# Sparse attention and a mixture of attention experts on one core: another order for all 766 steps

## The chip, the core and the metric

The kernel runs on one core of a Trainium2 chip. A core has five engines that run side by side, each through its own queue in order: TensorE (PE; its weight loads are shown as PEld), VectorE (DVE), ScalarE (ACT), GpSimd (POOL) and SyncE (SP), which only issues transfers here. DMA engines move data between memory and the core's SBUF; matmuls write to PSUM, eight banks of 512 fp32 per partition. The metric is the device time of one execution in microseconds (us). The profile comes from one execution; the times from three others.

## What is computed

```python
def _attn_ref(q, k, v):                 # (4, 8, 768, 64): batch, heads, positions, width
    block, window = (32, 16)
    k_sum = k.reshape(B, H, nb, block, D).max(axis=3)
    v_sum = v.reshape(B, H, nb, block, D).mean(axis=3)
    scores_l = scale * q @ k.T          # kept where |i - j| < window
    scores_s = scale * q @ k_sum.T + log(block)
    a = softmax(concat(scores_l_masked, scores_s))
    return a @ concat(v, v_sum)

def _moe_ref(x, w_gate, wq, wk, wv, wo):  # x: (4, 768, 512), E = 4 experts, 64 wide
    logits = x @ w_gate                   # the two largest of four, softmax over them
    for e in range(E):
        q, k, v = x @ wq[e], x @ wk[e], x @ wv[e]
        a = softmax(causal(scale * q @ k.T))
        out += weight_of(e) * (a @ v @ wo[e])
```

The second function takes the first one's output, heads side by side.

## The kernel before

The work is cut into 766 steps. `make_plan` declares them: a step has a name, the engines that it can run on, the buffers that it reads and writes, and a function that records its instructions. `TABLE` (from line 55) gives the order: each entry is a step's number, the engine that it runs on (P, V, A, G, S for PE, DVE, ACT, POOL, SP) and the slots of the buffers that it uses first. `Plan.emit` walks the table; so the table alone sets the order of every engine's queue, which copy of a tile or which PSUM bank a step uses, and through these every wait. `SLOTS` (line 51) says how many copies each tile has; PSUM has eight banks, and many steps take two at once.

Names of steps carry the batch b (0 to 3) and the pair of heads c (0 to 3), and for the second stage the pair of experts (0, 1) and a part. By pair of heads, in the first stage:

- dk, dq (POOL, lines 261 and 266) load k and q; dv (SP, lines 284 to 287) loads v into one of six `vb` tiles, in overlapping windows; hc copies the overlap within the tile.
- bs (line 304) sums v over blocks with matmuls against the selector `sel`, be adds up the parts and ds spreads the sums into `vb`. For the second half of the batches dvs loads v again and tr adds it up in a tree on POOL (line 347) in their place.
- tk and tq turn k and q with transposes on PE (line 366); kw and cq take them out of PSUM; rk takes the maximum over blocks and ksc spreads it.
- sc forms the scores (lines 414 and 420, the first adds the mask), ex takes the exponential on ACT (line 427), av multiplies by v (line 437), rc and xm divide (lines 448 and 452), tx turns the result (line 463), hi and lo keep it as a sum of two half-precision tiles (lo at line 482).

In the second stage, for a batch:

- vp forms v of all experts and the gate's logits (lines 554 and 557); v2 and lg take them out of PSUM; ga, gx, gb, gc work out the gate (lines 595 to 614).
- pp forms q and k of a pair of experts (line 630) and pc takes them out; sp forms a unit of scores (line 654), es takes the exponential (line 662, ACT), dm puts zeros above the diagonal (line 667, POOL), aw multiplies by v (line 678).
- r2 and wv divide and weigh (lines 697 to 704), tw turns (line 715), ct copies the turned tile `wT`, op multiplies by the output weights (line 737), oc takes the result out of PSUM into `ob`, od stores it (line 748).

The first stage of one batch is mixed with the second stage of the batch before it. The weights are loaded once (dw, dwv, dwo, dwg) and cast (cw, cvg, co, cg). 24 fillers fl (line 769) are steps that read zeros: on PE they are one or four matmuls of 512 columns, on ACT they record nothing. `vone`, `knz`, `kwz`, `id16`, `id32`, `idr`, `sel`, `mt`, `pi`, `vtz`, `v2o`, `zz` and `w1m` set constants before first use.

PE works in one of four array shapes: 128 rows by 128 columns (pp, vp, aw, op, fl), 64 by 128 (sc, sp, tx, tw), 128 by 64 (tk, tq, av; rows 100, 128 and 120 in the profile) and 128 by 32 (bs; 96 rows).

Plain copies and casts of all steps are recorded at line 168 when they run on ACT and at line 170 when they run on another engine, so one line of the profile holds many steps.

Of the kernel before, what the change touches and what calls it, by code (L numbers as in the profile page):

```python
# [15 lines left out]
S = 768  # L16
# [41 lines left out]
75,P,4.1 57,G, 56,A, 73,V, 94,P,6.0 232,G,2 49,P,5.1 72,V, 95,A, 67,G, 96,P,0.1 76,A, 126,P,2.2 50,V, 148,G, 74,A,  # L58
97,A, 77,P,6.2 127,A, 41,V,4 99,P,4.0.0 78,A, 109,P,3.0 234,S,4 68,P,2.0 51,A, 243,G,1 98,P, 69,V, 44,G, 62,G, 110,A,
105,P,0.2.2 79,P,6.3 236,S,3 107,V, 122,P,1.0.0 80,A, 70,G, 81,P,2.1.1 124,V, 106,A, 82,P, 100,V, 108,G, 101,V, 123,A,  # L60
233,G,2 252,P,6.1.1 83,V, 125,G, 111,P,4.4 84,V, 253,A, 0,G, 63,P,7.1 144,S,0 112,A, 128,P,0.5 64,V, 130,P,2.1 129,A,
143,S, 102,P,4.0.0 254,V, 131,A, 142,S,1 65,G, 113,P,0.0 269,P,7.0.2 103,V, 141,S, 132,P,2.0.2 270,A, 242,G,0 140,S,
104,V, 114,A, 145,S, 237,G, 271,V, 133,P, 85,P,4.1.1 235,G, 134,V, 135,V, 115,P,0.1.0 86,A, 116,P, 1,A, 87,V, 45,G,
136,P,6.2.2 117,V, 273,P,2.1 118,V, 137,A, 307,P,3.2 238,P,4.0 272,A, 138,V, 274,A, 150,G, 308,A, 275,P,0.2 239,V,
46,G, 119,P,6.3.3 276,A, 244,S,0 277,P,2.3 286,P,5.2.0 120,A, 240,G, 256,P,4.0 287,V, 278,A, 196,P,0.0 255,A, 241,G,
257,A, 288,V, 194,P,2.1 246,S,2 197,A, 121,V, 289,G, 149,G, 303,P,4.0.2 195,A, 290,P,5.1 304,V, 260,P,0.5 147,A,
204,P,6.0 408,S,0 279,P,2.0.1 406,S, 261,A, 305,V, 409,S, 280,P, 245,G, 205,A, 407,S, 152,P,0.0.0 402,S,3 281,V,
282,V, 291,A, 258,P,6.1 154,A, 283,P,4.4.4 259,A, 247,G, 153,V, 201,P,2 284,V, 202,A, 146,S, 306,G, 248,P,0.1 285,V,
401,G,1 203,G, 210,P,6 249,V, 198,P,2 263,P,4.1.2 199,A, 262,P, 251,G, 211,A, 165,P,0.2 404,S,4 264,V, 265,V, 415,G,2
# [12 lines left out]
226,P,4.4 230,A, 590,G,1 346,P,0.1 227,V, 343,P,6 347,A, 386,P,1.0.2 425,G,0 384,P, 344,A, 228,S, 385,P, 337,P,4
387,V, 604,P,0.1.0 338,A, 388,V, 349,P,6 466,P,1.2 350,A, 606,V, 352,P,4 427,G, 456,P,2.0.2 597,S,0 353,A, 467,V,
340,P,6 389,P,4.0 341,A, 455,P, 390,V, 345,G, 348,G, 483,P,1.1 605,A, 592,S,4 354,G, 457,V, 439,P,4.1.0 458,V, 465,G,
351,G, 438,P, 484,A, 339,G, 38,G,1 482,A, 468,P,6.2 440,V, 470,P,2.4 441,V, 469,A, 625,P,0.0 621,P,1.0.2 471,A, 626,V,
342,G, 487,P,6.0 580,S,1 426,G, 459,P,4.0.0 488,A, 622,V, 485,P,2.3 608,P,0.2 486,A, 355,P,0.1.6 607,G, 623,V, 357,P,
609,A, 593,G, 594,S,3 356,P, 460,A, 612,P,2.1 358,V, 489,P,0.0.1 417,G, 359,V, 613,A, 490,P, 461,V, 588,G, 360,P,2.1
624,A, 598,S, 442,P,6.1.1 596,S, 361,V, 629,P,4.5 231,S, 443,A, 491,V, 472,P,2.1.2 492,V, 599,S, 9,G, 630,A, 473,P,
444,V, 610,P,0.3 595,G, 493,P,4.2.2 474,V, 611,A, 475,V, 394,P,6.0 494,V, 579,G, 397,P,0.4 395,A, 495,V, 476,P,2.3.3
591,G,0 396,S, 391,P,6.2 477,A, 398,V, 540,P,4.1 392,A, 478,V, 399,S, 538,P,0.0 393,S, 541,A, 600,G, 627,P,6.0 539,V,  # L90
655,P,2.2.1 628,A, 638,P,3.1.0 656,V, 551,P,4.0 548,P,0 552,A, 589,G, 499,P,6.0.0 657,V, 549,A, 509,P,4.2 500,V,
601,G,0 639,V, 501,A, 554,P,0 510,A, 545,P,6 640,V, 642,P,2.1 555,A, 502,P,4 643,V, 546,A, 641,G, 496,P,0 553,G,
504,V, 550,G, 503,V, 581,G, 557,P,2 542,P,6 497,V, 498,V, 558,A, 644,P,4.2 543,A, 615,P,2.0.0 505,V,0.0 507,V, 614,P,
# [808 lines left out]
```

## Time and profile before

| | us |
|---|---|
| three runs | 165.97, 166.53, 166.67 |
| median | 166.53 |
| profiled execution | 162.94 |
| its span, from the first to the last instruction | 161.2 |
| PE busy in it | 143.5 |
| ACT busy | 119.5 |
| DVE busy | 116.8 |
| POOL busy | 109.9 |

The busy share of an engine is an average over the span. The slices of the page cut the span into 40 parts of 4.03 us; the chain follows the work that ended last back to the beginning. A row of grouped instructions has line, engine, operation, the tiles out<-in, their shapes, the count, then the busy time in us and the mean of one in ns, then the idle time of the engine before them and what ended it. A row of a timeline begins with the start in us and the length in us. The ends of matmuls are modelled: a matmul is shown as ending up to 0.17 us after the next one has begun.

### The profile page before, as it was taken

Reading aid. Unit: us, or ns where it says so; the run is one execution under the profiler, and the core shown is the slowest. Engines: PE = TensorE matmul, PEld = TensorE weight load, DVE = VectorE, ACT = ScalarE, POOL = GpSimd, SP = SyncE. Lnnn points to the kernel's source line nnn. Section 1 sums busy time; section 2 is a strip of 40 time slices with the busy share of each in tenths; the row PEclk is TensorE's granted clock in tenths of the full one; section 3 lists DMA queues with packets and bytes.
Section 4 is the critical chain, followed back from the end, with each engine's and each line's share of the span. In section 5 each row is a group of like instructions: output and inputs, shape, how many; then the busy total and the mean of one; then the engine's idle time right before and its main releaser. Section 6 shows DMA issues by size and latency. Waiting matters only on the chain.

```text
span 161.2 us, 6956 instructions
## 1 busy us (share of the span) xinstructions
PE 143.5 (89%) x2992; PEld 107.1 (66%) x2992; DVE 116.8 (72%) x236; ACT 119.5 (74%) x152; POOL 109.9 (68%) x184
## 2 busy tenths in 40 slices
PE   0049998769999999999999999998999998999994
PEld 0137796758687778577666988656778795466741
DVE  5527488985878967977786899968888578247940
ACT  0096999566996779898889997639788894999460
POOL 6987595984874999999999989649996230216100
PEclk9999999999999999999999999999999999999999
DMA  3999999997889996998799985699200000030746
GB/s 21 215 226 237 188 161 232 222 218 166 173 170 186 237 157 151 176 168 129 181 173 166 266 151 119 188 268 267 81 0 4 4 6 0 4 130 0 257 167 231
DMA packets 44158, 24.57 MB, mean 152 GB/s; under 512 B 33120, under 2 KB 40544, under 8 KB 43744
## 3 DMA queue, kind: packets, MB, share of 16 engines
q1 hardware_dynamic: 35552, 16.91, 43.7%
q0 software_dynamic: 7488, 6.29, 28.0%
q10 hardware_dynamic: 1088, 0.93, 1.7%
q8 instruction: 23, 0.38, 1.0%
q14 instruction: 7, 0.06, 0.1%
HBM read 24.13 MB, written 6.29 MB: 189 GB/s over the span
## 4 chain that ended last, share of the span: by engine, by line
PE 69%; ACT 12%; POOL 5%; issue 4%; DMA 4%; SPq 2%; DVE 2%; POOLq 0%; ACTq 0%; DVEq 0%
PE ps L437 13%; PE ps L630 12%; PE ps L554 6%; PE ps L678 6%; PE ps L654 6%; PE ps L366 6%; PE ps L737 4%; DMA out_dram<-ob 4%; PE ps L304 4%; PE ps L414 3%; PE ps L463 3%; ACT a L662 3%; PE ps L420 3%; ACT aT L427 2%; ACT kw L168 2%
## 5 line engine op out<-in xcount | busy, mean ns | idle before, releaser
L662 ACT ACTIVATE a<-ps 128x1024 f16<-128x1024 f32 (+1 forms) x48 | 41.7, 919 | 6.9 <-PE ps L654 4.9
L667 POOL TENSOR_SCALAR_AFFINE_SELECT a<-a 128x256 f16<-128x256 f16 x48 | 18.3, 406 | 22.1 <-ACT a L662 21.6
L427 ACT ACTIVATE aT<-ps 120x768 f32<-120x768 f32 x32 | 25.3, 812 | 4.5 <-PE ps L420 3.1
L437 PE MATMUL ps<-vb,aT 120*64 120x65 f32 x768 | 26.5, 224 | 1.3 <-issue 0.9
L437 PEld LDWEIGHTS ps<-vb,aT 120*64 120x64 f32 x768 | 24.1, 138 | 4.0 <-issue 2.4
L630 PE MATMUL ps<-hi,wqk 128*128 128x384 f16 x128 | 22.8, 326 | 0.3 <-ACT ob L168 0.3
L170 POOL COPY vb<-vb 32x1408 f32<-32x1408 f32 x15 | 20.1, 1350 | 3.7 <-DMA vb<-in_v_dram 3.1
L347 POOL TENSOR_TENSOR vt<-vt 120x1024 f32<-120x1024 f32 (+3 forms) x16 | 19.2, 1201 | 3.5 <-DMA vt<-in_v_dram 2.4
L630 PEld LDWEIGHTS <-wqk 128*128 128x128 f16 x128 | 11.7, 97 | 8.3 <-issue 1.0
L482 DVE TENSOR_TENSOR lo<-ps,hi 128x768 f16<-128x768 f32 x16 | 15.3, 955 | 1.3 <-ACT hi L168 0.8
L382 DVE TENSOR_REDUCE ks<-ps 128x24 f16<-128x768 f16 x16 | 15.0, 951 | 1.2 <-PE ps L366 1.0
L366 PE MATMUL ps<-idr,kn 100*64 100x100 f16 x256 | 8.9, 219 | 7.8 <-POOL idr L225 7.7
L452 DVE TENSOR_TENSOR x<-ps,rec 128x768 f32<-128x768 f32 x16 | 15.3, 958 | 0.6
L654 PE MATMUL ps<-qk,qk 64*128 64x512 f16 (+3 forms) x128 | 14.5, 307 | 0.7 <-ACT qk L168 0.4
L554 PE MATMUL ps<-wvg,hi 128*128 128x264 f16 x96 | 13.9, 276 | 0.1
L170 POOL COPY vb<-vu 24x768 f32<-24x768 f32 x16 | 13.1, 822 | 0.8
L366 PEld LDWEIGHTS <-kn 100*64 100x64 f16 x256 | 7.3, 117 | 9.0 <-DVE vb L210 5.6
L168 ACT COPY ob<-ps 128x1024 f32<-128x1024 f32 (+1 forms) x9 | 8.5, 968 | 6.1 <-PE ps L737 3.9
L170 POOL COPY vb<-vs 24x1536 f32<-24x1536 f32 x6 | 8.7, 1467 | 5.9 <-DVE vs L322 5.8
L678 PE MATMUL ps<-v,a 128*128 128x65 f16 x336 | 12.1, 193 | 0.0
L737 PE MATMUL ps<-wo,wT 128*128 128x512 f16 (+1 forms) x50 | 11.7, 371 | 0.4 <-DVE wT L170 0.4
L678 PEld LDWEIGHTS <-a 128*128 128x128 f16 x336 | 11.0, 97 | 1.5 <-issue 0.8
(95 smaller groups left out, 276.9 us busy)
## 6 DMA issues: line engine op xcount, KB each, us to landing
vb<-in_v_dram SPq DMA_DIRECT2D x32, 176.0 KB
out_dram<-ob SPq DMA_DIRECT2D x10, 512.0 KB
vt<-in_v_dram SPq DMA_DIRECT2D x16, 192.0 KB
kn<-in_k_dram POOLq DMA_DIRECT2D x6, 384.0 KB, 6.8
qn<-in_q_dram POOLq DMA_DIRECT2D x6, 384.0 KB, 6.6
kn<-in_k_dram POOLq DMA_DIRECT2D x4, 192.0 KB, 5.2
qn<-in_q_dram POOLq DMA_DIRECT2D x4, 192.0 KB, 5.9
a<-in_moe_wk_dram SPq DMA_DIRECT2D x2, 256.0 KB
```

What stands on the lines that cost most here:

```text
L170: en(e).tensor_copy(dst, src)
L347: en(e).tensor_tensor(y[0:120], x[0:120, 0:w], x[0:120, w:2 * w], AL.add)
L366: nc.tensor.transpose(dst[64 * hp:64 * hp + 64, p * s:p * s + p], src[:, hh + hp, 64 * s:64 * s + 64], idt)
L427: nc.scalar.activation(T["aT"][aT.slot][0:KR], pbank(sc, 2)[0:KR, :, 0:384], AF.Exp, scale=SCALE)
L437: nc.tensor.matmul(pbank(av, 2)[o:o + 64, u, 65 * (2 * (t // 2) + hp):65 * (2 * (t // 2) + hp) + 65], a[0:KR, hp, 64 * t:64 * t + 64], T[" ...
L554: nc.tensor.matmul(p[:, i, 0:264], hi_(ch)[:, cols], T["wvg"][:, ch, :], start=(ch == 0), stop=False, skip_group_check=True)
L630: nc.tensor.matmul(pbank(pp, 2)[:, u, 0:384], T["wqk"][:, cc, ch, j, :], hi_(ch)[:, 384 * u:384 * u + 384], start=(ch == 0), stop=(ch == N ...
L654: nc.tensor.matmul(pbank(sp, 2)[:, ep, c0:c0 + w], T["qk"][qk[1].slot][r, 128 * tj:128 * tj + 128], T["qk"][qk[0].slot][r, n0:n0 + w], sta ...
L662: nc.scalar.activation(a2v(u), pbank(sp, 2)[:, :, 0:ln], AF.Exp, scale=SCALE / (XS * XS))
L667: nc.gpsimd.affine_select(m, m, [[0, 2], [1, 128]], AL.is_ge, 0.0, base=0, channel_multiplier=-1)
L678: nc.tensor.matmul(pbank(av, 2)[:, ep, 65 * ti:65 * ti + 65], a2v(u)[:, ep, o:o + 128], T["v2"][v2.slot][:, tj, 2 * cc + ep, :], start=(tj ...
L737: nc.tensor.matmul(pbank(op, i1 - i0)[:, ti - i0, 0:n1 - n0], T["wT"][wTs[cc].slot][:, 128 * ti:128 * ti + 128], T["wo"][:, cc, n0:n1], st ...
```

## The change

Only the table is replaced. All 766 steps are there in both; every one of the lines differs. The first and the last lines:

```diff
 TABLE = """
-4,G,0 139,A, 40,V,3 2,G, 8,V, 52,S,3 39,G,2 35,G, 47,S,2 3,G,0 42,V,5 5,G, 58,G,1 6,G, 66,S,5 7,G, 34,V, 37,G,0
-88,P,0.0.0 53,A, 90,V, 60,G, 89,A, 59,G,1 61,S,0 43,G, 91,G, 54,P,1.0 36,G, 92,P,2.0 55,V, 48,G, 71,P,3.1.1 93,A,
...
-763,P,4.3 758,A, 23,P,5 761,V, 30,P,6 764,V, 29,P,7 759,A, 17,P,0 765,S, 16,A,1 762,A, 27,A,5 24,A,2 33,A,3 31,A,6
-14,A,7 15,A,4 18,A,1 32,A,1 13,A,1 28,A,1 21,P,1 22,P,2 19,P,3 10,P,4
+4,G,0 37,V,0 2,G, 5,G,0 40,V,3 52,S,0 3,G, 39,V,2 41,G,4 8,V, 47,S,3 57,G,1 59,G, 6,G, 43,G, 34,V, 66,S,2 7,G, 36,G,
+88,P,0.0.0 53,A, 90,V, 35,G, 58,G,1 42,G,5 91,A, 54,P,1.0 89,A, 71,P,2.1.1 55,V, 61,S,5 48,G, 92,P,3.0 73,V, 75,P,4.1
...
+717,V, 29,A,5 24,A,4 33,A,4 20,A,4 750,A, 26,P,4 30,A,5 18,A,5 757,P,5.6 756,S, 760,P,4.2 758,A, 763,P,6.3 28,P,7
+25,P,2 761,A, 764,V, 23,P,3 759,A, 19,P,0 765,S, 10,P,1 21,A,5 22,A,7 12,A,2 32,A,4 14,A,6 762,S, 15,P,3 17,P,2 13,P,4
 """
```

What the two tables say by engine, read with the names of the steps:

| queue | before | after |
|---|---|---|
| PE, begin | tk01 bs01 tq01 tk00 tq00 sc010 bs00 sc011 tq03 sc000 av011 | tk01 bs01 tk00 tq01 tq00 sc010 sc011 bs00 av010 sc001 tk02 sc000 |
| PE, end | op31 op30 tw311 tw301 op32 op33 op34, then 14 filler matmuls | op30 op31 tw311 tw301, 2 filler matmuls, op32 op33 op34, then 20 |
| POOL, begin | dk001 dk000 vone kwz dq000 dq001 dq010 id16 idr vone dq011 dk011 sel | dk001 dk000 dq001 dq000 vone dk010 dk011 id16 sel idr mt kwz dq010 |
| ACT, begin | dwg hc01 kw01 cq01 ds01 ex010 | hc01 ksc01 kw01 cq01 ksc00 ex010 |
| DVE, begin | vone knz vone pi rk01 be01 rk00 kw00 be00 | vone vone vone knz pi rk01 be01 rk00 cq00 ds01 kw00 be00 |
| SP, weights | dw11 dw10 dwv0 dw01 dw00 dwv1 in one row, dwo later | dwg dw11 dw10; after dv12 and dv13 dwo dwv0 dwv1; after dv23 and dvs203 dw00 dw01 |
| DVE, end | r2301 wv301 r2311 wv311 ct301 ct311 oc33 oc34 | r2311 r2301 wv311 wv301 oc31 ct301 oc34 |
| ACT, end | es310 gx3 oc21 oc22 es311 oc31 oc30 od30 oc32 od32 od33 | es310 gx3 es311 oc21 ct300 oc22 oc30 od30 ct311 oc32 oc33 od32 |

58 steps other than fillers run on another engine: kw13, kw20, kw31, kw33, hi01, hi12, hi23, pc000, pc101, pc210, pc310, cq22, cq31, v220, v231, ct210, ct300, ct311, oc12 and oc33 go from DVE to ACT; kw23, hi00, hi22, pc011, pc200, pc301, cq00, cq23, cq30, cq33, v200, v212, v221, ds01, oc20 and oc31 from ACT to DVE; hc03 and hc11 from POOL to ACT; ds12 from POOL to DVE; co, cvg and ds00 from ACT to POOL; ten copies ksc and four settings vone change places between POOL and ACT or DVE; dwg and od33 go from ACT's queue to SP's. Of the fillers six go to PE and four leave it, and so 22 filler matmuls are recorded where there were 14. Changes of PE's array shape from one step to the next number 119 before and 107 after.

More of the change, by code (lines that the diff above doesn't have):

```diff
@@ L106 @@
[L106 to L107 removed]
+4,G,0 37,V,0 2,G, 5,G,0 40,V,3 52,S,0 3,G, 39,V,2 41,G,4 8,V, 47,S,3 57,G,1 59,G, 6,G, 43,G, 34,V, 66,S,2 7,G, 36,G,
+88,P,0.0.0 53,A, 90,V, 35,G, 58,G,1 42,G,5 91,A, 54,P,1.0 89,A, 71,P,2.1.1 55,V, 61,S,5 48,G, 92,P,3.0 73,V, 75,P,4.1
+93,A, 60,G, 76,V, 74,A, 94,P,6.0 232,G,2 234,S,4 96,P,0.1 95,A, 56,V, 49,P,5.1 97,A, 72,V, 98,P,6.0.0 67,A, 50,V,
@@ new lines @@
+79,P,0.2 105,P,3.2.2 80,A, 107,V, 77,P,0.3 51,G, 122,P,4.0.0 78,A, 99,P, 124,V, 106,A, 108,G, 81,P,0.1.1 243,G,2
+236,S,0 100,V, 123,A, 44,G, 101,V, 125,G, 68,P,2.0 69,V, 62,G, 102,P,4.0.0 109,P,3.2 103,A, 82,P, 139,S, 110,A,
+126,P,6.0 83,V, 63,P,7.1 104,V, 127,A, 233,G,1 144,S,0 70,G, 84,V, 130,P,2.4 143,S, 113,P,4.5 131,A, 64,V, 85,P,0.1.1
+114,A, 128,P,2.0 252,P,6.1.1 86,V, 129,A, 65,G, 111,P,4.1 254,V, 132,P,2.0.2 112,A, 133,P, 242,G,1 237,A, 87,V, 235,G,
+269,P,7.0.2 244,S,2 134,V, 115,P,4.1.0 135,V, 270,A, 45,G, 116,P, 253,A, 271,V, 136,P,0.2.2 137,A, 117,V, 246,S,3
@@ new lines @@
+272,G, 118,V, 256,P,2.1 150,G, 138,V, 273,P,3.0 238,P,7.0 274,A, 0,G, 255,G, 257,A, 146,S,1 275,P,4.3 239,V, 277,P,0.2
+276,A, 119,P,2.3.3 142,S, 307,P,6.2 120,A, 241,G, 303,P,7.2.0 145,S, 194,P,4.0 308,A, 121,V, 278,A, 245,G, 305,V,
+286,P,6.0.2 195,A, 279,P,2.0.1 418,S,5 288,V, 306,G, 304,A, 290,P,0.0 148,G, 196,P,4.1 287,V, 291,A, 247,G, 309,P,0.0
+197,V, 258,P,6.4 409,S,0 310,A, 140,S, 280,P, 289,G, 46,G, 259,A, 141,S, 311,P,4.1 147,G, 281,V, 260,P,0.5 282,V,
+151,G, 408,S, 312,A, 292,P,6.3 261,A, 283,P,4.4.4 198,P,2.1 293,A, 240,G, 284,V, 248,P,0.1 406,S, 407,S, 199,A,
@@ new lines @@
+466,P,1.1 484,V, 456,P, 467,A, 349,P,2 457,V, 487,P,6.2 339,G, 350,A, 228,S, 458,V, 588,G, 608,P,0.2 621,P,1.2.1
+231,S, 609,V, 488,A, 485,P,4.3 389,P,2.0 486,A, 468,P,6.5 390,V, 342,G, 604,P,0.0.2 345,G, 623,V, 469,A, 348,G,
+352,P,2 459,P,4.0.0 351,G, 353,A, 470,P,6.4 606,V, 591,G,1 460,A, 356,P,1.1.2 354,G, 355,P, 471,A, 461,V, 624,G,
+357,P, 607,G, 622,A, 590,G,0 489,P,6.1.1 358,V, 417,G, 605,A, 359,V, 625,P,4.0 490,P, 626,A, 38,G,1 360,P,2.1 491,V,
+442,P,0.1.1 361,V, 629,P,4.1 443,A, 492,V, 394,P,2.0 630,A, 589,G, 592,S,1 444,V, 627,P,6.0 612,P,4.3 628,A,
@@ new lines @@
+472,P,0.0.2 581,G, 613,A, 473,P, 395,A, 597,S, 493,P,6.2.2 598,S, 474,V, 475,V, 391,P,4.4 596,S, 9,G, 494,A, 495,V,
+392,A, 397,P,2.2 476,P,0.3.3 398,A, 393,S, 610,P,6.2 477,V, 396,S, 642,P,4.1 611,A, 655,P,5.1.0 594,S,3 593,G,
+538,P,2.1 478,V, 656,A, 643,V, 579,G, 540,P,6.0 539,A, 399,S, 499,P,0.0.0 600,G, 541,A, 657,V, 557,P,2.1 558,A,
+548,P,4 501,V, 549,A, 659,P,6.0 638,P,7.2.1 500,V, 545,P,2 640,V, 551,P,0 546,A, 496,P,4 639,V, 552,A, 601,G,0
+509,P,2.2 497,V, 660,V, 498,A, 554,P,0 510,V, 542,P,4 555,A, 502,P,6 559,G, 543,A, 658,G, 511,P,2.0 503,V, 547,G,
@@ new lines @@
+565,P,0.0 670,A, 532,P, 534,V, 687,P,4.1 566,A, 671,V, 685,P,0.0 535,V, 688,V, 536,P,2.1 686,A, 537,V, 692,P,6.1
+704,P,4 689,P,0 705,A, 567,P,2.4 693,A, 718,P,4.2 690,A, 568,V, 694,G, 701,P,6 719,A, 569,S, 695,P,0 698,P,2 696,A,
+720,P,4.0 699,A, 675,P,0.1.1 721,V, 702,A, 731,P,2.0 677,A, 703,G, 728,P,4 725,P,6 700,G, 732,A, 676,V, 691,G, 678,P,0
+697,G, 729,A, 672,P,2 680,V, 726,A, 730,G, 679,V, 733,G, 737,P,4 722,P,0 706,G, 673,V, 674,V, 738,A, 734,P,6 11,A,4
+723,A, 739,G, 681,V,4.1 570,P,2.0 682,A, 735,A, 724,G, 708,P,0.0.0 683,V, 727,G, 707,P, 684,V, 16,A,5 571,A,
```

70 lines of the change are left out of this document (22 added, 48 removed).

## The prediction

> **What bounds the kernel now.** I read the page first (busy shares, slices, chain), then the busy time of four stretches, then TensorE's waits, then the timelines of the start and of the end.
>
> ```profile
> span 161.2 us, 6956 instructions
> PE 143.5 (89%) x2992; PEld 107.1 (66%) x2992; DVE 116.8 (72%) x236; ACT 119.5 (74%) x152; POOL 109.9 (68%) x184
> PE   0049998769999999999999999998999998999994
> ...
> q8 instruction: 23, 0.38, 1.0%
> ...
> PE 69%; ACT 12%; POOL 5%; issue 4%; DMA 4%; SPq 2%; DVE 2%; POOLq 0%; ACTq 0%; DVEq 0%
> ```
>
> TensorE (PE) is 89% busy, and the slices show that its idle time lies at the start; 69% of the chain that ended last is its work. The same by stretches (start, middle, entry to the end, end; the first column after the stretch is its length, then PE busy):
>
> ```profile
> 0.00:28.48 28.48, 17.57 (x461) 14.48 (x462) 17.51 (x46) 18.31 (x20) 21.32 (x56) 1.00 1.07 182
> 28.48:130.37 101.89, 98.73 (x2188) 75.57 (x2184) 82.55 (x146) 81.61 (x108) 83.15 (x115) 1.00 0.79 159
> 130.37:142.06 11.69, 10.92 (x149) 6.98 (x149) 6.32 (x11) 8.76 (x12) 1.62 (x4) 1.00 0.07 23
> 142.06:161.20 19.14, 16.26 (x208) 10.09 (x206) 10.40 (x35) 10.86 (x14) 3.78 (x10) 1.00 0.41 154
> ```
>
> In the middle PE is idle for 101.89 - 98.73 = 3.2 us of 102. So an order can gain there only by making PE's own work shorter, and can lose there by new waits; start and end have more to give. What PE waited for:
>
> ```profile
> PE ps L304 <- POOL sel L244: 2.2, 1, 2.2
> PE ps L366 <- issue: 1.3, 1, 1.3
> PE ps L437 <- issue: 0.9, 1, 0.9
> ...
> PE ps L414 <- ACT ob L168: 0.6, 1, 0.6
> ```
>
> The two "issue" waits (2.2 us) are two thirds of the middle's idle time; nothing that the profile shows ended them. The rest, some 1.0 us, are evacuations that came late.
>
> **The change part by part.** The same 766 steps are emitted in another order, 58 of them (and ten fillers) on another engine, with other buffer slots. No matmul of the result is added or removed, so PE's work stays, but for three things: changes of array shape, fillers, and waits.
>
> *Shape changes.* Each PE row names its array shape (128\*128, 64\*128, 128\*64 and so on). Where it stays, a group starts 0.17 us before the end of the one before; where it changes, 0.07 us:
>
> ```profile
> 68.59 0.49 PE L630 MATMUL ps<-hi,wqk 128*128 128x384 f16 x2
> 68.91 1.68 PE L678 MATMUL ps<-v,a 128*128 128x65 f16 x50
> 70.53 0.61 PE L654 MATMUL ps<-qk,qk 64*128 64x512 f16 x6
> 71.07 1.21 PE L678 MATMUL ps<-v,a 128*128 128x65 f16 x34
> 72.21 0.39 PE L654 MATMUL ps<-qk,qk 64*128 64x512 f16 x2
> ```
>
> 68.59 + 0.49 = 69.08 against 68.91 is 0.17 (no change); 70.59 against 70.53 and 72.28 against 72.21 is 0.06 to 0.07. A change costs 0.10 us. Counting them in the two step lists by these shapes (100, 120 and 128 rows by 64 columns as one) gives 119 before and 107 after. Of the 12, the middle (from step av030 to av330) has 11 fewer (83 against 72), the start one more, the end two fewer. Middle: 11 x 0.10 = -1.1 us, if nothing else ends a wait there. Bounds: -1.1 and 0.
>
> *Start.* These rows carry it:
>
> ```profile
> 6.98 0.62 POOL L225 COPY idr<-id 100x2 f16<-100x2 f16 x3
> 8.42 1.28 ACT L168 ACT_TABLE_LOAD   x1 [8.42 <-DMA vb<-in_v_dram]
> 9.71 1.36 ACT L168 COPY vb<-vb 32x1408 f32<-32x1408 f32 x1
> 10.46 0.18 POOL L244 TENSOR_SCALAR_AFFINE_SELECT sel<-sel 96x2 f32<-96x2 f32 x1
> ```
> ```profile
> 10.70 1.92 PE L304 MATMUL ps<-vb,sel 96*32 96x128 f32 x24 [2.16 <-POOL sel L244]
> ...
> 14.65 0.50 PE L414 MATMUL ps<-pi,mt 64*128 64x384 f16 x2
> ...
> ...
> 16.60 0.34 PE L414 MATMUL ps<-pi,mt 64*128 64x384 f16 x2
> ```
>
> The first block sums (bs01) wait 2.16 us for `sel`, which POOL builds last, though their data had landed by 8.42 (the load of the activation table started then). After, `sel` stands ahead of `idr`: POOL's queue is then four loads' issues, one `vone`, two more loads, `id16`, `sel`, `idr`; by the rows of these steps `sel` is done near 8.0 and `idr` near 8.7. So the first transposes (tk01) start 1.0 us later, at 8.7, and bs01 behind them at 9.5 instead of 10.70. That isn't all gain: the first scores (sc010) still need hc01 on ACT, which ends at 9.71 + 1.36 = 11.07, then kw01 and cq01. ACT's queue puts sc010 near 13.6 against 14.65. The kw00 copy and the be00/ds00 sums behind it add about 0.5 us of waiting at sc000 (its bank waits for ex001, queued behind hc03 and so behind that load), and PE then works on without a hole. I get the step av030 at 27.5 instead of 28.48: -1.0 us, bounds -1.3 (bs01's own shift) and 0 (the load lands a microsecond later, because the queue now issues four loads by 4.3 us where before two were held back).
>
> PE is also slow here: the two rows of L414 take 0.50 and 0.34 us for the same work. The Trainium skill ("TensorE: Matmul & The Clock Gate", What's actually happening) says that an array that was idle runs at half rate for about 3.4 us of sustained work, in a window that runs free of the kernel. The rows show the slow rate lasting until about 16.5, almost 6 us after 10.70; by the skill's figure the gain could be an estimated 1 us larger, or gone, with the window's phase.
>
> *End.* The entry (av330 to the last qk projection) has the same steps on PE and comes out even, within 0.1 us, by the rows. Behind it:
>
> ```profile
> 152.49 1.89 PE L737 MATMUL ps<-wo,wT 128*128 128x512 f16 x8
> ...
> 154.64 0.49 DVE L170 COPY wT<-ps 128x256 f16<-128x256 f16 x2 [0.73 <-PE ps L715]
> 154.99 1.04 PE L737 MATMUL ps<-wo,wT 128*128 128x512 f16 x6 [0.39 <-DVE wT L170]
> ...
> 156.56 1.17 ACTq L748 DMA_DIRECT2D out_dram<-ob  x2
> 156.69 0.35 SPq L748 DMA_DIRECT2D out_dram<-ob  x1
> ```
> ```profile
> L170 DVE COPY ob<-ps 128x1024 f32<-128x1024 f32 x3 | 3.7, 1221 | 1.3 <-PE ps L737 1.3
> ```
> ```profile
> 156.03 3.02 PE ps L769 x14
> ```
>
> Before, op31 and op30 end at 152.49 + 1.89 = 154.38, DVE turns to ct301 at once, and op32 starts at 154.99, 0.6 us later. After, DVE's order is oc31, then ct301: the copy of 1.22 us comes first, then the 0.28 us half of the wT copy. op32 then starts 1.5 us after op31: +0.9. Two shape changes fewer: -0.2. The last store moves from ACT's queue, where two issues took 1.17 us, to SP's (0.35): -0.3. Fillers: 14 matmuls stood behind the last product, 3.02 us; after there are 20, 4.3 us, which end some 0.3 us after the stores would: +0.3. End: +0.7, bounds 0 (the fillers stay hidden and PE fills the wait) and +2.0 (aw310's bank also waits for es311 on ACT).
>
> *Steps that change engines.* hc03 and hc11 go from POOL to ACT; co, cvg, ds00 leave ACT for POOL; ds01 goes from ACT to DVE; five evacuations kw, the projections' copies, ct, hi and v change between DVE and ACT.
>
> ```profile
> L168 ACT COPY kw<-ps 128x1152 f16<-128x1152 f16 x9 | 9.8, 1119 | 0.4 <-DVE ks L382 0.4
> ...
> L168 ACT CAST qk<-ps 128x768 f16<-128x768 f32 x11 | 8.8, 804 | 3.5 <-PE ps L630 3.3
> ```
>
> ACT's whole load rises by under 1 us, but it loses work in the first 45 us and gains about 4.0 after them: two kw net (2.2), two pc net (1.6), three ct (an estimated 1.8 from the qk row by width), less 1.6 of the others. I cost it at nothing: ACT is busy 81.61 of the middle's 101.89 us and its copies lie beside PE's matmuls. If that cover goes, it costs up to half of it, 2.0 us (next part). The loads keep their lead: the block rows of v that arrive latest relative to their use (dv32, dk210) are still issued 7 to 8 us ahead, counted in PE's rows.
>
> Sum against the profiled execution, 162.94 us (span 161.2 and 1.7 around it): -1.0 - 1.1 + 0.7 = -1.4, so 161.5. The three runs shown have a median of 166.53, 3.6 above the profiled one, and the profile can't show what lies between; I carry the difference over: 166.53 - 1.4 = 165.1 us.
>
> **The rivals.**
> *ScalarE becomes the pace in the middle (slower).* For it:
>
> ```profile
> 64.00:80.00 16.00, 15.63 (x300) 10.93 (x297) 13.14 (x20) 14.09 (x19) 15.07 (x23) 1.00 0.96 165
> 80.00:96.00 16.00, 16.00 (x371) 12.23 (x369) 13.18 (x28) 14.50 (x20) 15.03 (x27) 1.00 1.00 187
> ```
>
> Here ACT is busy 14.09 + 14.50 = 28.6 of 32 us, and a bank that it frees late stops PE at once (0.6 us behind `ob` above). New tight spots of that kind are tx13 behind es005 and av320 behind es205: 1.02 us of exp plus the hand-off against about 0.5 us of PE work between. Price: the shape saving is lost as waiting, and half of ACT's 4.0 us comes on top: -1.0 + 2.0 + 0.7 = +1.7, 168.2 us. It decides once PE's waits for evacuations in the middle pass 2.4 us: today's 1.0, the 1.1 of the shapes, and the 0.3 by which the start's gain exceeds the end's loss. Against it: PE idles 3.2 us in 102 with an ACT no less busy. The Trainium skill ("TensorEngine Tiling (Array Packing)", PSUM Bottleneck) says that packing the array speeds up matmuls but not the evacuation of PSUM; by that rule this case would be the likeliest; the trace shows PE at 16.00 of 16 beside ACT's 14.50, which doesn't bear it out.
>
> *The instruction stalls go (faster).*
>
> ```profile
> 28.65 0.48 PE ps L437 x14
> 29.12 0.88 issue
> 30.00 1.26 PE ps L437 x34
> ...
> 34.58 1.26 issue
> ```
>
> In both, PE stops in the middle of a group, some 250 instructions apart; 2 x 2992 PE instructions over the 23 packets of the instruction queue are 260 each. So PE ran out of instructions while the loads held the DMA engines. If the new order's loads (the weights come in three lots instead of one) let both packets through: -1.4 - 2.1 = -3.5, 163.0 us. Against it: both orders have 256-instruction stretches of 4 to 5 us there. The opposite, two more such stops, is +2.1 and lies inside the range.
>
> *The start's gain isn't kept (no change).* Then -1.1 + 0.7 = -0.4, 166.1: bs01 starts early, but sc000 and av000 wait for the same loads as before.
>
> **How the numbers follow.** Forecast 0.40; ScalarE 0.32; no instruction stalls 0.10; no change 0.18. A difference under 0.5%, 0.8 us, is about what a measurement here can't tell from none. Faster: nine tenths of 0.40, and 0.10, with a little of the last case: 0.47. Same 0.18, slower 0.35. The forecast's own range, from the bounds of its terms that are most alike, is 164.0 to 166.4; with the rivals on both sides 162.7 to 168.6.
>
> **What would show it.** Right: the first L304 row of PE starts near 9.5; the wait for `sel` is gone from PE's waits; PE busy in the middle falls by about 1 us at the same count; op32's wait names DVE and is over 1 us. Wrong: waits of PE for ACT over 2.4 us in the middle; av030 not before 28.2; "issue" waits that add up to more than 4 us or to none; an end stretch over 20.5 us.

## The result, and the profile after

| us | before | after |
|---|---|---|
| median (runs) | 165.97 (5: 165.41 to 166.67) | 168.63 (5: 167.66 to 172.22) |
| profiled execution | 162.94 | 168.63 |
| its span | 161.2 | 166.9 |

The changed kernel is slower: the ratio is 1.038, 95% interval 1.033 to 1.043. This ratio and those below are taken over the quicker executions of each kernel, so they can differ from the ratio of two medians. Here the five times of the kernel before lie above its level: 168.63 / 1.038 is 162.5, near the profiled 162.94, and beside the experiments its median was 162.6 to 163.5 in 7 to 29 runs.

The page of the changed kernel (span, busy times, slices of PE, instruction queue, chain):

```profile
span 166.9 us, 6976 instructions
PE 145.7 (87%) x3000; PEld 107.9 (65%) x3000; DVE 117.1 (70%) x233; ACT 120.4 (72%) x153; POOL 110.4 (66%) x186
PE   0038889989975999999999998999999998999987
...
q8 instruction: 23, 0.38, 1.0%
...
PE 3%; issue 0%
```

PE is no busier in share; the slices show a later start (3 where there was a 4) and a hole in the 13th slice, near 50 us. The chain says little here: it ends in the fillers behind the last product and is followed back for 3% of the span only. The same four stretches as before (length, then PE, PEld, DVE, ACT, POOL busy):

```profile
0.00:30.93 30.93, 17.78 (x456) 14.22 (x457) 20.49 (x49) 16.45 (x20) 20.20 (x51) 1.00 0.95 158
30.93:135.15 104.22, 99.09 (x2188) 75.90 (x2190) 79.76 (x143) 84.88 (x108) 85.62 (x124) 1.00 0.80 158
135.15:146.71 11.56, 10.77 (x145) 6.89 (x145) 7.01 (x11) 7.62 (x10) 0.41 (x1) 1.00 0.13 48
146.71:166.90 20.19, 18.05 (x217) 10.88 (x214) 9.87 (x32) 11.46 (x17) 4.20 (x11) 1.00 0.35 131
```

Against 28.48, 101.89, 11.69 and 19.14 these are +2.45, +2.33, -0.13 and +1.05, together +5.70. The prediction had -1.0, -1.1, 0 and +0.7. What PE waited for:

```profile
PE ps L304 <- ACT vb L168: 1.8, 1, 1.8
PE ps L437 <- issue: 1.5, 1, 1.5
PE ps L304 <- DMA vb<-in_v_dram: 1.4, 1, 1.4
PE ps L420 <- issue: 1.0, 1, 1.0
PE ps L366 <- issue: 0.7, 1, 0.7
PE ps L737 <- DVE wT L170: 0.7, 1, 0.7
...
PE ps L678 <- POOL a L667: 0.5, 1, 0.5
...
PE ps L437 <- POOL vb L170: 0.4, 1, 0.4
```

The wait for `sel` is gone, and two others stand in its place at the same line: the first block sums wait for their v load itself and for the copy hc01 that follows it (1.4 + 1.8 us). In the middle PE stopped three times for "issue", that is, for nothing that the profile shows (3.2 us against 2.2; such pauses are called stops below), and waited 0.9 us for POOL, for which it did not wait there before. At the end there is a wait for DVE's copy of `wT`.

The start of the changed kernel, as a timeline:

```profile
2.79 1.43 POOL L266 DMA_DIRECT2D qn<-in_q_dram  x2
...
6.27 2.77 SPq L287 DMA_DIRECT2D vb<-in_v_dram  x1
...
10.32 1.28 ACT L168 ACT_TABLE_LOAD   x1 [10.32 <-DMA vb<-in_v_dram]
...
11.61 1.36 ACT L168 COPY vb<-vb 32x1408 f32<-32x1408 f32 x1
...
13.03 1.50 PE L304 MATMUL ps<-vb,sel 96*32 96x128 f32 x22 [1.77 <-ACT vb L168]
```

ACT's table load stands behind the wait for the first v load, dv01, so its start is the landing: 10.32 us, where it was 8.42. The copy hc01 and then the second part of bs01 (22 of its 24 matmuls) follow one behind the other. Two q loads are issued from 2.79 us on, and SP's issue of a v load at 6.27 us takes 2.77 us where the one before (at 6.82) took 0.67. The end:

```profile
159.11 1.22 DVE L170 COPY ob<-ps 128x1024 f32<-128x1024 f32 x1 [0.39 <-PE ps L737]
...
160.25 0.28 DVE L170 COPY wT<-ps 128x256 f16<-128x256 f16 x1
...
160.59 1.04 PE L737 MATMUL ps<-wo,wT 128*128 128x512 f16 x6 [0.69 <-DVE wT L170]
...
161.47 4.48 PE L769 MATMUL ps<-zz 128*128 128x512 f16 x20
```

DVE takes oc31 first (1.22 us), then its half of `wT`; op32 starts at 160.59, 1.51 us after op31's end at 159.08 (0.61 before). PE filled part of that gap with two fillers, so the wait that it shows is 0.69 us.

### The profile page after: what moved, and what is told of

Same layout as the page of the kernel before. It is cut to its first block, busy times and chain, and to the rows that moved or that the text cites. A ratio compares the mean times of both kernels' runs of the same rounds, so it can differ in the third digit from the quotient of the medians.

```text
span 166.9 us, 6976 instructions
## 1 busy us (share of the span) xinstructions
PE 145.7 (87%) x3000; PEld 107.9 (65%) x3000; DVE 117.1 (70%) x233; ACT 120.4 (72%) x153; POOL 110.4 (66%) x186
## 5 line engine op out<-in xcount | busy, mean ns | idle before, releaser
L667 POOL TENSOR_SCALAR_AFFINE_SELECT a<-a 128x256 f16<-128x256 f16 x48 | 18.4, 409 | 20.8 <-ACT a L662 20.0
L437 PE MATMUL ps<-vb,aT 120*64 120x65 f32 x768 | 27.3, 224 | 3.1 <-issue 1.5
L437 PEld LDWEIGHTS ps<-vb,aT 120*64 120x64 f32 x768 | 24.6, 138 | 6.4 <-issue 3.4
L347 POOL TENSOR_TENSOR vt<-vt 120x1024 f32<-120x1024 f32 (+3 forms) x16 | 19.8, 1239 | 2.6 <-DMA vt<-in_v_dram 1.6
L170 POOL COPY vb<-vb 32x1408 f32<-32x1408 f32 x13 | 17.5, 1350 | 4.1 <-DMA vb<-in_v_dram 3.5
L654 PE MATMUL ps<-qk,qk 64*128 64x512 f16 (+3 forms) x128 | 13.6, 306 | 0.7 <-DVE wT L170 0.7
L678 PE MATMUL ps<-v,a 128*128 128x65 f16 x336 | 12.6, 193 | 0.7 <-POOL a L667 0.5
L168 ACT COPY kw<-ps 128x1152 f16<-128x1152 f16 x12 | 13.2, 1128 | 0.0
L168 ACT CAST qk<-ps 128x768 f16<-128x768 f32 x12 | 9.6, 800 | 4.3 <-PE ps L630 4.0
```

The source lines that it names most:

```text
L168: nc.scalar.copy(dst, src)
L170: en(e).tensor_copy(dst, src)
L347: en(e).tensor_tensor(y[0:120], x[0:120, 0:w], x[0:120, w:2 * w], AL.add)
L437: nc.tensor.matmul(pbank(av, 2)[o:o + 64, u, 65 * (2 * (t // 2) + hp):65 * (2 * (t // 2) + hp) + 65], a[0:KR, hp, 64 * t:64 * t + 64], T[" ...
L667: nc.gpsimd.affine_select(m, m, [[0, 2], [1, 128]], AL.is_ge, 0.0, base=0, channel_multiplier=-1)
L678: nc.tensor.matmul(pbank(av, 2)[:, ep, 65 * ti:65 * ti + 65], a2v(u)[:, ep, o:o + 128], T["v2"][v2.slot][:, tj, 2 * cc + ep, :], start=(tj ...
```

## The experiments

The before of each comparison ran on the same chip as the kernel. None leaves out any work of the result. In the diffs, a line is a queue, with the names of its steps.

**The q loads at the start.** a_qlate, from the changed kernel:

```diff
-POOL: dk001 dk000 dq001 dq000 vone4 dk010 dk011 id16 sel idr mt kwz dq010
+POOL: dk001 dk000 vone4 kwz dq001 dq000 dk010 dk011 id16 sel idr mt dq010
```

> The changed kernel with two of GpSimd's steps moved in its queue: the issues of the q loads dq001 and dq000 stand behind vone4 and kwz, so 1.4 us later, where the kernel before had them. Theory (the start is late because the early q loads hold up dv01, the first v load): dv01's wait on ScalarE ends near 8.4 us instead of 10.3, the first block sums (bs01) end near 12.6 instead of 14.5, the step av030 starts 1.5 to 2 us earlier than 30.9, and the whole is 1.5 to 2 us shorter. Rival (the landing of dv01 varies by itself, or the two k loads hold it up): the wait still ends after 9.8 us and the time stays within 0.5 us.

```profile
4.19 1.42 POOL L266 DMA_DIRECT2D qn<-in_q_dram  x2
...
7.98 1.28 ACT L168 ACT_TABLE_LOAD   x1 [7.98 <-DMA vb<-in_v_dram]
...
9.28 1.36 ACT L168 COPY vb<-vb 32x1408 f32<-32x1408 f32 x1
...
9.63 0.64 PE L304 MATMUL ps<-vb,sel 96*32 96x128 f32 x2
10.69 1.50 PE L304 MATMUL ps<-vb,sel 96*32 96x128 f32 x22 [0.42 <-ACT vb L168]
```

This timeline of a_qlate shows the loads issued 1.4 us later and dv01 landed 2.34 us earlier, at 7.98. The step av030, with which the middle begins, comes at 28.55 in place of 30.93. The ratio to before is 1.020 (1.010 to 1.031; 167.28 us against 162.89). So the start's loss against the kernel before was the place of two loads in POOL's queue.

The rows show one thing more. PE starts bs01 at 9.63 without a wait, as predicted, but the second part waits for hc01, so bs01 ends at 12.19, 0.44 us earlier than before, and that is how much earlier dv01 landed. The first scores follow at 14.21 in place of 14.65, and av030 at 28.55 in place of 28.48. The earlier `sel` alone brought nothing here: behind it stood hc01, which follows the landing, the table load and its own 1.36 us.

b_qearly puts the same two loads early in the kernel before and changes nothing else:

```diff
-POOL: dk001 dk000 vone2 kwz dq000 dq001 dq010
+POOL: dk001 dk000 dq001 dq000 vone2 kwz dq010
```

> The kernel before with one thing of the change alone: the loads of dq001 and dq000 are issued on GpSimd right behind dk000. Theory that these loads delay the first v load: ScalarE's table load, which waits for dv01's landing, starts at 9.9 to 10.9 us in place of 8.42, the first matmuls of bs01 end 1 us later or more than 12.63, and the time rises by 1.5 to 2.5 us (164.5 to 165.5 by the profile). Rival, that the start of the changed kernel was late for another reason (the order of the other loads): dv01 lands within 0.5 us of 8.42 and the time stays within 0.5 us.

```profile
6.78 2.66 SPq L287 DMA_DIRECT2D vb<-in_v_dram  x1
...
10.74 1.28 ACT L168 ACT_TABLE_LOAD   x1 [10.74 <-DMA vb<-in_v_dram]
```

dv01 landed at 10.74 (expected 9.9 to 10.9), bs01 ended at 14.96 in place of 12.63, av030 came at 30.82; the same long issue on SP is there. The time rose by 1.1% (ratio 1.0115, with an interval, 1.000 to 1.023, that just reaches no change; 165.97 us against 163.34). Both directions agree. Over all profiles, with the two loads at 2.8 us dv01 landed between 10.32 and 11.34 (six profiles), with them at 4.2 us between 7.86 and 9.68 (eleven).

The DMA queues show what the loads took. By their sizes, q0 carries the loads of k and q that POOL issues, and q1 the loads that SP issues; dv01 is 0.39 MB (2 heads of 768 by 64 in fp32). Between 4 and 8 us:

| | before | a_qlate | changed | b_qearly |
|---|---|---|---|---|
| q0, packets' time as a share of 16 engines | 72.6% | 76.1% | 87.3% | 88.1% |
| q1, MB moved | 0.39 | 0.41 | 0.27 | 0.26 |
| dv01 landed at, us | 8.42 | 7.98 | 10.32 | 10.74 |

In the six profiles with the early loads q1 moved 0.23 to 0.27 MB in these 4 us, in the eleven others 0.39 to 0.41. So the early q loads held the DMA engines while dv01's data were due. No run shows which packet waited for which.

a_table makes ACT load its table before the landing (`at`, an activation of line 757 on the constant `w1m`):

```diff
-ACT: hc01 ksc01 ...      DVE: vone0 vone3 ...
+ACT: at hc01 ksc01 ...   DVE: w1m vone0 vone3 ...
```

> The changed kernel with w1m first on VectorE and the one-element exponential `at` first on ScalarE, so that the load of the activation table (1.28 us) doesn't stand between the landing of dv01 and the copy hc01. Theory (bs01 waits for hc01 on ScalarE): hc01 and all behind it start 1.3 us earlier, bs01 ends 1.3 us earlier, and the whole is 0.8 to 1.3 us shorter. Rival (the start is overtaken later by other waits): hc01 earlier, but av030 less than 0.4 us earlier and the time within 0.5 us.

167.64 us, ratio 1.034 (1.025 to 1.042), not separate from the changed kernel's. hc01 began at its load's landing, but that was 11.33 in this profile, a microsecond later than in the changed kernel's; av030 came at 30.69. Counted from the landing, av030 comes 19.36 us later here, and 20.61 and 21.49 us later in the changed kernel's two profiles (the second follows below). So the move is worth 1.25 us or more at this place, and the later landing took most of it away.

b_start gives the kernel before the earlier `sel` of the change together with a_table's early table load, which the change does not have, and leaves the order of its first loads alone:

```diff
-POOL: ... id16 idr vone0 ... dk011 sel       ACT: dwg hc01 ...      DVE: vone3 ...
+POOL: ... id16 idr sel vone0 ... dk011       ACT: at dwg hc01 ...   DVE: w1m vone3 ...
```

> The kernel before with the gain that the change was to bring at its start and without its order of loads: w1m first on VectorE, the last of the early GpSimd constants behind it, and the load of sel ahead of vone0. Theory that bs01 waits only for what is ready first: bs01 starts at 9.5 us or before (10.70 before), hc01 ends within 1.5 us of dv01's landing near 8.4 us, av030 comes 0.8 to 1.3 us before 28.48 and the time falls by about 1 us (161.9 by the profile). Rival, that the gain is overtaken by the loads behind it: av030 within 0.3 us of 28.48 and the time within 0.3 us.

```profile
8.52 1.36 ACT L168 COPY vb<-vb 32x1408 f32<-32x1408 f32 x1 [6.21 <-DMA vb<-in_v_dram]
8.80 0.60 PE L304 MATMUL ps<-vb,sel 96*32 96x128 f32 x2 [0.26 <-DMA vb<-in_v_dram]
```

hc01 starts with the landing, bs01 at 8.80 in place of 10.70, and av030 comes at 27.28, 1.2 us earlier. The time was 161.70 us against 163.34: ratio 0.984 (0.971 to 0.997). The kernel was run once more beside another version:

> The kernel b_start again, beside a_best on one chip: the kernel before with only the changed kernel's gain at the start (w1m first, sel ahead of vone0). Theory: about 1.2 to 1.6 us under the kernel before, with an interval that leaves out 1. If the remedies of a_best hold, a_best is 0.5 to 1.5 us under it; if stops at issue belong to the changed order, b_start5 is the faster.

162.06 us against 163.47, ratio 0.994 (0.990 to 0.999) in 12 runs against 29. By its medians it is the quickest kernel here, 1.6 and 0.6% under the kernel before in its two comparisons. No run has the two moves of b_start apart. By the rows each alone would end bs01 where it ended: with `sel` early it waits for hc01 (a_qlate), with the table early it would still wait for `sel` at 10.64.

**The end.** a_nofill puts all 24 fillers on ACT, where they record nothing:

> The changed kernel with all 24 fillers as steps without instructions (no matmul of zeros at the end). Theory (SyncE's last wait, 165.02 to 165.99 us, is for the 20 fillers behind the last product): 0.9 us shorter, nothing else moves. Rival (the stores set the end anyway): within 0.3 us.

The four executions took 336.54, 168.11, 171.97 and 168.61 us; ratio 1.035 (1.027 to 1.042). The profile is that of the first, in which PE was busy for 317.8 us, so it tells nothing of the end. The time shows no gain. a_tail also puts the two halves of `wT` first on DVE:

```diff
-ACT: ... oc30 od30 ... ct311 ... oc32 oc33 od32      DVE: ... wv301 oc31 ct301 oc34
+ACT: ... oc30 oc31 od30 ... oc32 od32                DVE: ... wv301 ct301 ct311 oc33 oc34
```

> As the kernel without fillers, and the end's copies on the engines that the kernel before had: oc30 then oc31 on ScalarE, ct301 and ct311 on VectorE straight after the transposes, oc33 on VectorE. Theory (oc31's 1.22 us ahead of ct301 on VectorE holds up op32): op32 starts 0.6 to 0.7 us after op31's end instead of 1.5, and the whole is 0.6 us shorter than without fillers alone, 1.5 shorter than the changed kernel. Rival (the last stores set the end whichever copy comes first): op32 earlier by 0.7, the end not.

```profile
157.62 1.93 ACT L168 COPY ob<-ps 128x1024 f32<-128x1024 f32 x2 [1.11 <-PE ps L737]
...
158.71 0.49 DVE L170 COPY wT<-ps 128x256 f16<-128x256 f16 x2 [0.61 <-PE ps L715]
...
159.06 1.04 PE L737 MATMUL ps<-wo,wT 128*128 128x512 f16 x6 [0.39 <-DVE wT L170]
```

op32 follows op31's end (158.45) by 0.61 us, not 1.51: the 0.9 us are DVE's order. From the end of av330 to the last instruction a_tail takes 30.84 us, the changed kernel 31.77 and the kernel before 30.86. From op34's end to the last instruction a_tail takes 5.25 us without fillers, the changed kernel 5.29 with 20 of them: the fillers cost nothing that the profiles show. The whole time (168.08 us, ratio 1.031, 1.024 to 1.037) doesn't separate from the changed kernel's, for in this profile dv01 landed at 11.34.

**The middle: loads, GpSimd, instruction stops.** a_loads (with a_qlate's start) tests whether PE runs out of instructions because loads hold the DMA engines:

```diff
-SP: ... dwv1 dv23 dvs203 ... dvs201 dv30 dv21 ... dv20 dvs212     POOL: ... ds10 hc23 cw0 ... hc21 ksc23
+SP: ... dwv1 dvs203 ... dvs201 dv21 ... dv20 dv23 dv30 dvs212     POOL: ... ds10 cw0 ... hc21 hc23 ksc23
```

> The changed kernel with the three q loads 1.4 us later, and in the middle the loads dv23 and dv30 issued later on SyncE (behind dv20) and hc23 later on GpSimd. Theory that instruction packets come late because the loads of the middle hold the DMA engines: the stops of TensorE at issue near sc101 and av100 (1.65 and 0.89 us in a_qlate) fall below 0.5 us each, and the span falls by 1.5 to 2.0 us from 163.2. Rival, that the packets are late whatever these two loads do: stops of more than 2 us in sum remain in the middle and the span stays within 0.5 us of 163.2.

166.66 us, ratio 1.019 (1.012 to 1.025), as a_qlate. The two stops at sc101 and av100 were gone, but others were longer (1.5 us at tq11) and "issue" summed to 2.9 us between 26 and 137 us, against 3.0 in a_qlate. Neither side is borne out by this one profile. A second profile of the changed kernel itself shows how far such stops vary:

> One more look at the changed kernel itself. Theory that its first v load is late by the order of GpSimd's loads: dv01 lands at 10.0 us or later again and av030 comes at 30 us or later; TensorE's waits for GpSimd and its stops at issue between 26 and 137 us sum to 3.5 us or more again (4.1 in its first profile). Rival, that the first profile was an odd one: dv01 before 9.5 us, or that sum under 2.5 us.

It took 169.28 us; dv01 landed at 10.94 and av030 came at 32.43. Of PE's waits between 28 and 135 us none is for issue. The waits for POOL:

```profile
PE ps L678 <- POOL a L667: 2.4, 3, 1.3
...
PE ps L437 <- POOL vb L170: 0.7, 1, 0.7
```

The stretch from av030 to av330 took 103.37 us, within 0.9 of the profile with three stops. One profile has 3.2 us of stops and 0.9 of waits for POOL, the other none and 3.1 (and 0.9 for a q load); all waits of PE between 26 and 137 us sum to 5.1 and 5.0. Stops and waits for POOL together, 3.1 us, stayed under the 3.5 expected.

In these two profiles the stops took the place of waits. Three more have the same order in the middle (a_table without `at` and w1m there). In a_qlate stops and waits for POOL are 3.0 and 0.5 us, in a_table 0.7 and 2.4, in a_tail 0.4 and 1.3. Where the stops are long the waits are short, but the sum is not fixed: it runs from 1.7 to 4.1 us, and the middle from 101.93 us in a_tail, no longer than before, over 102.84 and 102.90 to 104.22. So the +2.33 us of the first profile are the upper end of a spread, and a stop replaces a wait only in part. The timeline of the second profile near 88 us shows where PE waits for POOL:

```profile
86.02 1.68 POOL L170 COPY vb<-vu 24x768 f32<-24x768 f32 x2
86.28 0.38 ACT L662 ACTIVATE a<-ps 128x256 f16<-128x256 f32 x1 [1.67 <-PE ps L654]
87.78 2.35 POOL L347 TENSOR_TENSOR vt<-vt 120x1024 f32<-120x1024 f32 x1
...
90.09 0.40 POOL L667 TENSOR_SCALAR_AFFINE_SELECT a<-a 128x256 f16<-128x256 f16 x1
...
90.55 0.54 PE L678 MATMUL ps<-v,a 128*128 128x65 f16 x12 [1.32 <-POOL a L667]
```

ACT has the exponentials ready at 86.66. POOL masks them (dm115, 0.40 us) at 90.09, behind two copies and a tree sum, and PE waits 1.32 us for it. a_pool (with a_qlate's start) takes two such steps out of the way:

```diff
-POOL: ... ds20 tr210 dm115 tr211 ... dm100 ds30 dm102 ... dq310 dm105 ksc31
+POOL: ... ds20 dm115 tr210 tr211 ... dm100 dm102 ... dq310 dm105 ds30 ksc31
```

> The changed kernel with the three q loads 1.4 us later (as in a_qlate), and on GpSimd two evictions put ahead: dm115 before the reduction tr210, and ds30 behind dm105. Theory that GpSimd's order sets the middle: the matmuls aw101, aw102 and aw112 waited 0.23, 0.68 and 0.2 us or more for GpSimd's evictions; these waits fall below 0.3 us in all and the span is about 1.0 us under that of a_qlate (163.2 us), so 162.2. Rival, that other waits take their place (TensorE is within a few tenths of the other engines everywhere): the span stays within 0.3 us of 163.2.

165.92 us in ten runs, ratio 1.010 (1.002 to 1.019), nine thousandths under a_loads beside it; the intervals overlap. The profiled execution is one of the longest (168.98) and has 3.6 us of stops, so its waits can't be compared. To have it without the other two losses, a_best joins a_qlate's start (with id16, idr and sel ahead of dk010), a_table, a_tail and a_pool; a_best_np is the same without a_pool's moves:

> The changed kernel with all the remedies at once: the two q loads 1.4 us later, w1m first on VectorE, idr and id16 ahead of the second k loads, GpSimd's dm115 and ds30 put ahead, the tail with both ct copies on VectorE and oc30, oc31 on ScalarE, no filler matmuls. If the slowdown is the sum of these three places (the first v load, GpSimd's queue in the middle, VectorE's order at the end), the start ends near 27.5 us (av030), no wait for GpSimd over 0.2 us is left in the middle, and the stretch from the last 128-wide reduction's end to the end is 0.9 us shorter; with the 1.1 us of array shapes kept the time comes to 1.5 to 3.0 us under the kernel before, apart from stops at issue. Rival, that stops at issue belong to this order whatever is done around it: the time is not under that of the kernel before by more than 0.5 us, and the trace shows more than 4 us of stops.

> The same without the two GpSimd moves (dm115, ds30). Theory that GpSimd's queue cost the middle about 1 us: 0.8 to 1.3 us slower than a_best, with waits of aw101, aw102 and aw112 for GpSimd of 0.9 us or more in sum. Rival, that other waits take their place: within 0.3 us of a_best.

a_best 162.70 us, ratio 0.998 (0.993 to 1.002); a_best_np 164.11 us, ratio 1.009 (1.005 to 1.014). The two moves are worth 1.4 us by the medians and 1.2% by the ratios, whose intervals do not overlap. With the three places mended and b_start's gain added the changed order is level with the kernel before, so most of its 3.8% lay there. Step by step the ratios, each to the kernel before on the same chip, are 1.038, 1.020 with the q loads back, 1.009 with the start and the end mended as well, 0.998 with the two moves. Its own expected gain of 1.5 to 3.0 us under before didn't come, and b_start5 beside it, which a_best was to beat by 0.5 to 1.5 us, was 0.6 us quicker (the intervals overlap). In the profile of a_best the start ends at 27.75, 0.7 earlier, but the middle takes 102.32 us and the end 19.26: there the shapes' saving is still spent on waits.

Whether the 1.4 us are POOL's waits the first profiles leave open (the longer one has 3.7 us of stops and 0.2 of waits for POOL), so each has a second one:

> One more look at a_best_np. Theory that GpSimd's queue is the pace of its middle: the waits of TensorE for GpSimd and the stops at issue sum to 3.5 us or more between 26 and 137 us again (3.9 in its first profile), whatever the share of each, since a stop only takes the place of a wait. Rival, that stops at issue of 3 us or more belong to this order: they are 3 us or more again.

> One more look at a_best. Theory that GpSimd's queue is the pace without the two moves: the two sums together are 2.5 us or less here (2.5 in its first profile), 1 us or more under those of a_best_np. Rival, that stops at issue decide: the sum goes with the stops, and these differ between the two looks by more than 1 us.

In a_best_np's second profile stops (1.9) and waits for POOL (0.5) sum to 2.4 us, not the 3.5 expected, in a_best's to 2.3, where 1 us less was expected. So these sums do not explain the difference. But a_best_np's middle is 2.3 us longer (103.66 against 101.36), and PE was busy 1.8 us more for the same 2188 matmuls (100.28 against 98.46). The windows of a_np_look (PE busy is the second figure, the granted clock stands behind POOL) show why:

```profile
32.80:34.60 1.80, 0.30 (x12) 0.14 (x6) 1.77 (x4) 0.56 (x1) 0.42 (x1) 1.00 0.65 130
34.60:36.60 2.00, 1.95 (x37) 1.86 (x41) 0.50 (x1) 1.50 (x2) 1.53 (x3) 0.64 0.61 139
36.60:38.60 2.00, 2.00 (x40) 1.28 (x31) 0.73 (x3) 0.12 (x1) 0.00 (x0) 0.50 0.76 167
38.60:40.60 2.00, 2.00 (x58) 1.67 (x55) 0.84 (x3) 1.94 (x3) 1.41 (x1) 1.00 0.73 212
```

A stop of 1.55 us for issue near 33 us is followed by 3.4 us at half clock (for 1.44 of the 2 us at a mean of 0.64, then for 2 us). That lies more than 50 us ahead of the two moved steps, so it isn't their doing. Nor does it carry the difference in the times: the mean granted clock of the twelve executions is 0.990 for a_best_np and 0.992 for a_best. Of the 1.4 us, PE's waits for POOL's masks (L667) account for about 0.5 (aw102 waited 0.52 us in a_np_look, not at all in a_best_look); the rest stays open. a_best2 moves one more mask, dm105, ahead of the load dq310 that it stood behind:

> a_best with one more move: GpSimd's dm105 ahead of the load dq310, which it stood behind while aw102 waited 0.66 us for it. Theory that GpSimd's queue is the pace of the middle: that wait falls below 0.2 us and the time lies 0.4 to 0.8 us under a_best (median 162.7, ratio 0.9975). Rival, that stops at issue decide: within 0.3 us of a_best.

162.76 us, ratio 1.001 (0.995 to 1.008): no gain. aw102's wait (0.49 us in a_best's first profile) is gone, but aw012 waited 0.51 us for POOL instead. The time is the rival's. That stops decide is not shown by it (1.2 us of them in this profile); a third mask moved in POOL's queue brings nothing that can be measured.

## Why the prediction was wrong

*Start.* The step that failed is the value taken there, "-1.0 us", with 0 as its worst bound; +2.45 was measured. It failed twice.

First, the gain. The prediction has bs01 "at 9.5 instead of 10.70" and from that the first scores "near 13.6 against 14.65". a_qlate, with the loads back in place, has bs01 at 9.63, and yet the scores at 14.21 and av030 at 28.55: +0.07 against the kernel before. The prediction counted hc01 as needed for the first scores. It left out that the second part of bs01 itself waits for hc01, and that the transposes ahead of the scores stand behind bs01 in PE's queue. Only with the table load moved too did the gain come (b_start, 1.2 us).

Second, the load. The bound named the right thing, "the load lands a microsecond later, because the queue now issues four loads by 4.3 us", but I took it as unlikely and as costing only the gain. The landing moved by 1.9 us in the first profile and 2.5 in the second, and everything behind it, hc01 and the second part of bs01, moved with it: from 28.55 to 30.93, 2.38 us. a_qlate and b_qearly show that this is the loads' order. The profile of before had a warning: the DMA engines were full then (in the first stretch the time of their packets sums to 1.07 of the 16 engines').

The clock's part is small: in a_qlate, with bs01 from 9.63, the rows of L414 take 0.50 us at 14.21 and 0.33 at 14.77, so the slow rate ended 5 us behind bs01, against almost 6 before.

*Middle, shapes.* The term -1.1 was right in its mechanism, as far as the rows show it. Counted over PE's steps from av030 to av330, 91 begin 0.17 us before the end of the one ahead and 71 begin 0.07 us before it, where it was 82 and 82; all overlaps sum to 19.8 us against 18.9, so 0.9 us were saved. The sign that I named for it, PE busy 1 us less, didn't come (99.09 and 98.51 us in the two profiles, 98.73 before); other steps in the stretch (sp201 and tk11 come in, tx00 goes out) may be part of that, the rest isn't explained. In the first profile the 0.9 us and 2.3 more went into waits.

*Middle, engine changes at nothing.* This is the second step that failed. I named "ACT is busy 81.61 of the middle's 101.89 us" as the cover and ScalarE as the rival. PE's waits for ACT stayed at 0.4 to 0.7 us there. The engine for which PE waited more was POOL (nothing there before, 0.9 and 3.1 us in the two profiles), and the rows quoted for ScalarE had it: 15.07 and 15.03 of 16 us busy, more than ACT's 14.09 and 14.50. POOL's busy time in the middle rose only from 83.15 to 85.62 us; what PE waits for is a mask of 0.4 us behind 4 us of copies and sums in its queue. Two moved steps gave 1.4 us, of which the profiles account for 0.5. The term itself is sized only roughly: the middle took 0.0 to 2.3 us more than before in five profiles of this order.

*Instruction stops.* Kept as they were in the sum; by the profiles 3.2 and 0 us in two executions of one kernel, 0 to 3.7 over all versions of its order and 0.9 to 2.4 over four profiles of the kernel before and its versions. The bounds for them, 2.1 us less or 2.1 more, held to a tenth, but a stop isn't a term by itself where another wait would have come in its place. That stops are instruction packets held up by loads, as the prediction has it, no run shows: a_loads moved two loads away and the stops summed to 2.9 us in place of 3.0.

*Entry* came out even, as predicted (-0.13).

*End.* +1.05 against +0.7: oc31 ahead of ct301 cost the predicted 0.9, and a_tail, with the old order of these copies and no fillers, got the whole loss of entry and end back (30.84 us against 31.77). The fillers' +0.3, the store's -0.3 and the shapes' -0.2 don't show.

*The base.* I carried the 3.6 us between the profiled execution and the median of three over to the forecast. Later medians of 162.6 to 163.5 say that the profiled 162.94 was the kernel's level. Without it the forecast would have been 161.5; that the forecast of 165.1 lies as near to 168.63 as it does is luck: the profile's own difference is +5.7 us against -1.4.

*The signs.* Of those named for a wrong forecast, "av030 not before 28.2" came in both profiles of the changed kernel and "issue" waits adding up to none in the second. The waits for ACT and the end stretch stayed under their limits (0.7 of 2.4 us, 20.19 of 20.5).

## What to carry to other kernels

Where the DMA engines are full, as in this start, ask which load pays for one that is moved ahead, and look at the landing of the load that the first work waits for. When a wait is taken away, follow the step to its end: the next wait may stand right behind (here hc01 behind `sel`). In a hand-written order, look for short steps behind long ones in the busiest queue of each stretch; the busy sums don't show them. And before a stop or wait is counted as a loss or a gain, take more than one profile: here one order's middle took from 101.93 to 104.22 us.

## What was unexpected in the hardware

- *Half clock after a short stop.* The clock fell to 0.50 after PE idled 1.5 of 1.8 us (a_np_look, above). The Trainium skill ("TensorE: Matmul & The Clock Gate", Part 1) has the array go back to half rate after an idle window of about 3.4 us; here an idle time of half of that was followed by it, in some runs. A stop of 2.6 us in a_best_np's first profile was followed by 6.6 us at half clock. After the changed kernel's own stop of 1.5 us near 53 us the clock stayed at 1.00.
- *A long execution.* One execution in four of a_nofill took 336.54 us, with a granted clock of 1.00 in its record and PE busy for 317.8 us. No run shows its cause.
- *The landing varies.* With the same order of the first loads (a_qlate, a_loads, a_pool) dv01 landed at 7.98, 8.69 and 9.68 us.
